# Granule 3's averages transposed by DMA in place of TensorE, granule 7's loads released by these transposes, and steps 8 and 9 reordered

## The chip, the cores and the metric

One core of a Trainium2 chip runs the whole program. The metric is device time in microseconds (us), lower is better. Each execution is listed with its span (first to last event in the trace) and its mean granted TensorE clock. The time is about 1.8 us longer than the span.

## The reference

Attention with a global and a local window and a linear bias, then a two-layer MLP with a squared ReLU:

```python
# q, k, v: (4, 8, 768, 64) fp32, n_global 8, n_local 96
rel = pos[:, None] - pos[None, :]
keep = (pos[None, :] < n_global) | ((rel >= 0) & (rel < n_local))
scores = q @ k.T / sqrt(64) - slope[h] * dist       # -1e9 where not keep
a = softmax(scores)
x = (a @ v) -> (3072, 512)                          # heads side by side
h = x @ w_in                                        # 512 -> 2048
g = s * relu(h)**2 + b
out = g @ w_out                                     # 2048 -> 512
```

## The kernel before

The 3072 tokens go in 12 granules of 256 tokens (2 blocks of 128). A granule needs, in order: loads of k, q, v (GpSimd), their transposes (the first granules on TensorE, the later ones by DMA), scores (TensorE), exponentials (ScalarE), masks (VectorE), attention (TensorE), normalised averages `xn` (VectorE), the averages transposed to `xT`, and the two layers of the MLP. Instructions stand in a hand-written order on each engine; a "step" is half a granule of attention with MLP work of earlier granules mixed in.

`xT` is made in one of two ways, chosen by `X_PE`, and the end of a granule releases the loads of the granule four later:

```python
QK_PE = 4
X_PE = 4          # granules below this: transposes on TensorE
LEAD = 4
...
def x_by_pe(j, evac=(nc.vector.tensor_copy, nc.scalar.copy)):
    t = xT_tile(j)
    for e, ev in enumerate(evac):                      # cut: sizes
        ps = ps_h.tile([P, nk, GT], BF16, name="ps_x", tag="psh")
        ...
        nc.tensor.transpose(ps[:, kc, ...], xn[j][:, i, c : c + P], ident_bf[:])   # 4 per evac
        ev(t[:, e * nk : (e + 1) * nk, :], ps[:])

def x_by_dma(j):
    t = xT_tile(j)
    for i in range(GB):                                # 2
        nc.sync.dma_start_transpose(t[:, :, i * P : (i + 1) * P], xn[j][:, i, :])

def hold_loads(ap):                                    # GpSimd waits until ap is there
    g = work.tile([P, 1], BF16, name="gate", tag="gate")
    nc.gpsimd.tensor_copy(g[0:1, :], ap)

def finish_granule(j):
    if j < X_PE:
        x_by_pe(j)
    else:
        x_by_dma(j)
    while stores:
        stores.pop(0)()
    if 6 <= j + LEAD < NJ:
        hold_loads(xT[j][0:1, 0, GT - 1 : GT])         # the gate
        load_granule(j + LEAD)
```

So the gate of granule 3 is a one-element copy on GpSimd, and everything that GpSimd does after it, granule 7's loads first, waits for `xT` of granule 3. The place of the change in the order of instructions:

```python
make_koff(4)                     # VectorE: shifted keys "ko" of granule 4
run(p1[2][6:8])
finish_granule(3)
run(scores(8))                   # granule 4; half of them read ko
make_voff(4)
p2_mm(2, 0, 0, FC // 2)
...
def step(s, c0, c1, c2, pool=None, pre=()):
    ...
    posts = scores(s + 1)
    run(exps); run(pre); run(masks)
    run(c0)
    stage_A(2 * s); flush()          # attention of two pairs of heads
    ...
    run(c1)
    stage_A(2 * s + 1, pool); flush()
    n = 2 if j < X_PE else 1
    run(c2[0:n])
    if last: finish_granule(j) ...
    run(c2[n:]); flush()
```

`late_p1(3, ...)` and `act_p1(3, ...)` are first-layer groups of granule 3 (8 matmuls, a ReLU on ScalarE, a square on VectorE or, in `act_p1`, on ScalarE). `sg_sum` and `weight_sums` are sums and differences that VectorE prepares for a product scheme with fewer matmuls, `sg_prod` these products.

The softmax here doesn't subtract the row's maximum and nothing guards it: scores larger than these inputs give would overflow.

## Time and profile before

| | before |
|---|---|
| time, median of 3 (lowest to highest) | 207.94 us (207.74 to 208.59) |
| span of the profiled run | 206.1 us |
| TensorE, VectorE, ScalarE, GpSimd busy | 98, 80, 63, 34 % |
| granted TensorE clock | 1.0 |

The prediction shows the busy table, the chain and the queues. Three more things are needed. The first is how busy the 16 DMA engines are over the whole span, in the page's row of 40 slices (5.15 us each, a digit is tenths):

```profile
DMA  5999999999999999999999999994360300340006
```

In the slices up to about 139 us (27 of them, all but the first at 90% or more) DMA has next to no room. The second is the view of the tile `xT` in the kernel before, whose transposes of granules 4 to 11 all go by DMA:

```profile
DMA to landing us min/median/max: 2.4/4.9/8.3
```

The third is the timeline of the kernel before, where the columns are start, busy time, engine, line, operation, and the idle time before it with what ended it. The gate of granule 3 is passed early, and the second attention group of step 10 (line 504) waits 0.24 us for VectorE:

```profile
61.75 0.18 POOL L122 COPY gate<-xT 1x1 bf16<-1x1 bf16 x1
...
81.05 0.29 PEld L504 LDWEIGHTS <-pt 128*128 128x128 bf16 x8 [0.24 <-DVE xn L469]
```

### The profile page before, as it was taken

Reading aid. Unit: us, or ns where it says so; the run is one execution under the profiler, and the core shown is the slowest. Engines: PE = TensorE matmul, PEld = TensorE weight load, DVE = VectorE, ACT = ScalarE, POOL = GpSimd, SP = SyncE. Lnnn points to the kernel's source line nnn. Section 1 sums busy time; section 2 is a strip of 40 time slices with the busy share of each in tenths; the row PEclk is TensorE's granted clock in tenths of the full one; section 3 lists DMA queues with packets and bytes.
Section 4 is the critical chain, followed back from the end, with each engine's and each line's share of the span. In section 5 each row is a group of like instructions: output and inputs, shape, how many; then the busy total and the mean of one; then the engine's idle time right before and its main releaser. Section 6 shows DMA issues by size and latency. Waiting matters only on the chain.

```text
span 206.1 us, 5375 instructions
## 1 busy us (share of the span) xinstructions
PE 201.6 (98%) x2209; PEld 162.5 (79%) x2214; DVE 164.8 (80%) x347; ACT 129.3 (63%) x200; POOL 70.2 (34%) x90
## 2 busy tenths in 40 slices
PE   8999999999999999999999999999999999999993
PEld 2678885557876588888888898888888889888883
DVE  6877689979989999999699865699866696737974
ACT  5767669585975668885763694763694754476200
POOL 8986333899555601808301908200000000000000
PEclk9999999999999999999999999999999999999999
DMA  5999999999999999999999999994360300340006
GB/s 156 177 178 201 207 206 180 155 153 131 126 143 125 156 125 229 117 168 188 145 272 192 131 173 202 180 192 78 54 207 3 101 4 0 69 138 0 3 7 197
DMA packets 110836, 28.17 MB, mean 137 GB/s; under 512 B 97852, under 2 KB 109308, under 8 KB 110812
## 3 DMA queue, kind: packets, MB, share of 16 engines
q0 software_dynamic: 76000, 13.11, 87.9%
q1 hardware_dynamic: 33612, 14.13, 39.9%
q10 hardware_dynamic: 1200, 0.59, 1.1%
q8 instruction: 17, 0.28, 0.5%
q14 instruction: 7, 0.06, 0.1%
HBM read 27.26 MB, written 6.29 MB: 163 GB/s over the span
## 4 chain that ended last, share of the span: by engine, by line
PE 95%; DMA 2%; DVE 0%; ACT 0%; issue 0%
PE ps L632 41%; PE ps L832 24%; PE ps L680 10%; PE ps_s L444 6%; PE ps_av L504 5%; PE ps L968 3%; DMA first<-in_k_dram 2%; PE ps_s L530 1%; PE ps_t L354 1%; PE ps_s L419 1%; PE ps_x L604 1%; PE ps_s L545 1%; PE ps_t L331 1%; PE ps_av L571 1%; PE ps_t L344 0%; PE ps_last L832 0%
## 5 line engine op out<-in xcount | busy, mean ns | idle before, releaser
L632 PE MATMUL ps<-xT,w_in_bf 128*128 128x256 bf16 x768 | 90.4, 273 | 0.0
L642 ACT ACTIVATE gT<-ps 128x512 bf16<-128x512 f32 x96 | 55.8, 598 | 46.0 <-PE ps L632 45.8
L632 PEld LDWEIGHTS <-w_in_bf 128*128 128x128 bf16 x768 | 73.0, 98 | 9.2 <-DVE xT L607 0.2
L453 ACT ACTIVATE pt<-ps_s 128x1024 bf16<-128x1024 f32 (+1 forms) x44 | 39.3, 946 | 2.9 <-PE ps_s L444 2.8
L832 PEld LDWEIGHTS <-gsum 128*128 128x128 bf16 x256 | 24.2, 98 | 3.7 <-DVE gsum L795 0.5
L460 DVE TENSOR_TENSOR pt<-pt,tmpl 128x1024 bf16<-128x1024 bf16 (+1 forms) x40 | 24.4, 644 | 2.1 <-ACT pt L453 2.0
L108 POOL DMA_DIRECT2D vb<-in_v_dram x24 | 21.6, 914 | 5.3 <-DMA w_out_bf<-in_moe_w_out_dram 3.3
L806 DVE TENSOR_TENSOR gT<-gT 128x1024 bf16<-128x1024 bf16 x20 | 13.7, 687 | 11.6 <-ACT gT L642 11.6
L680 PE MATMUL ps<-w_out_bf,gT 128*128 128x512 bf16 x91 | 21.8, 379 | 0.3
L469 DVE TENSOR_TENSOR xn<-ps_av,rc 128x256 bf16<-128x256 f32 x48 | 20.4, 425 | 1.7
L832 PEld LDWEIGHTS <-gT 128*128 128x128 bf16 x200 | 18.6, 98 | 2.3
L504 PEld LDWEIGHTS <-pt 128*128 128x128 bf16 x320 | 14.4, 97 | 2.8 <-DVE xn L469 0.9
L680 PEld LDWEIGHTS <-gT 128*128 128x128 bf16 x96 | 8.9, 98 | 9.6
L468 DVE RECIPROCAL rc<-ps_av 128x4 f32<-128x4 f32 x48 | 8.6, 179 | 9.1 <-PE ps_av L504 7.8
L504 PE MATMUL ps_av<-vb,pt 128*128 128x65 bf16 x208 | 15.5, 193 | 0.0
L832 PE MATMUL ps<-w_out_bf,gsum 128*128 128x256 bf16 x128 | 15.3, 273 | 0.0
L832 PE MATMUL ps<-wsub,gsum 128*128 128x256 bf16 x128 | 15.1, 273 | 0.0
L116 POOL DMA_DIRECT2D nat<-in_q_dram x14 | 12.5, 890 | 6.9 <-DMA nat<-in_q_dram 2.9
L645 DVE TENSOR_TENSOR gT<-gT 128x512 bf16<-128x512 bf16 x30 | 12.2, 421 | 3.2 <-ACT gT L642 2.7
L122 POOL COPY gate<-xT 1x1 bf16<-1x1 bf16 x6 | 1.9, 314 | 36.1 <-DMA xT<-xn 36.1
L116 POOL DMA_DIRECT2D nat<-in_k_dram x14 | 12.6, 900 | 4.7 <-DMA w_in_bf<-in_moe_w_in_dram 2.5
L832 PE MATMUL ps<-w_out_bf,gT 128*128 128x256 bf16 x120 | 13.9, 273 | 0.0
(124 smaller groups left out, 249.7 us busy)
## 6 DMA issues: line engine op xcount, KB each, us to landing
out_dram<-o_q SPq DMA_DIRECT2D x15, 256.0 KB, 2.6
vb<-in_v_dram POOLq DMA_DIRECT2D x24, 128.0 KB, 7.6
nat<-in_k_dram POOLq DMA_DIRECT2D x22, 128.0 KB, 6.8
nat<-in_q_dram POOLq DMA_DIRECT2D x22, 128.0 KB, 6.9
w_out_bf<-in_moe_w_out_dram POOLq DMA_DIRECT2D x4, 512.0 KB, 16.1
w_in_bf<-in_moe_w_in_dram POOLq DMA_DIRECT2D x4, 256.0 KB, 7.6
w_in_bf<-in_moe_w_in_dram POOLq DMA_DIRECT2D x2, 512.0 KB, 11.1
out_dram<-o_sb SPq DMA_DIRECT2D x4, 256.0 KB
```

Of the source, the lines that this page charges most:

```text
L108: nc.gpsimd.dma_start(vbuf[b % 2][:, sb, :, 0:D], rows_of(v, b, sb))
L116: nc.gpsimd.dma_start(t[:, n, i, :, :], rows_of(srcs[n], b, sb))
L444: nc.tensor.matmul(ps[:, hi, oc * P : (oc + 1) * P], lhsT=kt[rows], rhs=qt[rows], start=not bias, stop=not bias or part * GB + n == len(pl ...
L453: nc.scalar.activation(pt[:, :, 0:ncol], ps[:, :, 0:ncol], ACT.Exp, scale=QSCALE)
L460: nc.vector.tensor_tensor(pv, pv, m.rearrange("p h a c -> p h (a c)"), ALU.mult)
L469: nc.vector.tensor_tensor(dst, av[:, :, :, 0:D], rc[:].to_broadcast((P, 2, 2, D)), ALU.mult)
L504: nc.tensor.matmul(av[:, i, hi, 0 : D + 1], lhsT=pt[:, hi, c * P : (c + 1) * P], rhs=vv, start=(n == 0), stop=(n == len(terms) - 1),)
L632: nc.tensor.matmul(ps[:, i, :], lhsT=w_in_bf[:, kc, fc * P : (fc + 1) * P], rhs=xT[j][:, kc, :], start=(kc == 0), stop=(kc == KC - 1),)
L642: nc.scalar.activation(gs, ps[:], ACT.Relu)
L680: nc.tensor.matmul(po[:], lhsT=g_of(j)[:, fc, tb * P : (tb + 1) * P], rhs=w_out_bf[:, fc, :], start=(fc == 0), stop=(fc == FC - 1),)
L806: outs.append(lambda: nc.vector.tensor_tensor(gs, gs, gs, ALU.mult))
L832: nc.tensor.matmul(ps[:, tb, cs], lhsT=stat[:, fc, tb * P : (tb + 1) * P], rhs=mov[:, fc, cs], start=(fc == 0), stop=(fc == NH - 1),)
```

## The change

Intent: TensorE is the bound, so its 8 transposes of granule 3 go to the DMA queue, which serves the later granules already. Because the DMA takes longer, the first-layer groups of granule 3 move from steps 8 and 9 to step 9 alone, and second-layer matmuls of granule 2 fill step 8. The gate then opens only when these transposes have landed.

```diff
-    X_PE = 4
+    X_PE = 3
...
-    step(8, [lambda: rest(2, 0)] + late_p1(3, (0,)), late_p1(3, (1, 2)), late_p1(3, (3,)))
+    step(8, [lambda: rest(2, 0)], [lambda: p2_mm(2, 1, 0, FC // 2)], [lambda: rest(2, 1)])
     step(
         9,
-        [weight_sums[1]] + p2[2][1:2],
-        [sg_sum(3)] + act_p1(3, (4, 5)),
-        late_p1(3, (6,)) + [weight_sums[2]] + late_p1(3, (7,)) + [flush, sg_sum(1)],
+        late_p1(3, (0, 1)),
+        [weight_sums[2]] + late_p1(3, (2, 3)),
+        act_p1(3, (4, 5)) + [flush, sg_sum(3)] + late_p1(3, (6,)) + [weight_sums[1]] + late_p1(3, (7,)) + [flush, sg_sum(1)],
     )
     step(
         10,
         [sg_prod(7), sg_prod(1), sg_prod(2)],
         [bias_diff, lambda: shifted_template(range(H)), sg_prod(5)],
-        [sg_sum(4)],
-        pre=[sg_sum(2)],
+        [sg_sum(4)], pre=[sg_sum(2)],
     )
```

## The prediction

> **What bounds the kernel now.** I read the page's busy table first, then the chain of work that ended last in order of time, then the timeline of single engines around the place that changes, and last the DMA queues there.
>
> ```profile
> PE 201.6 (98%) x2209; PEld 162.5 (79%) x2214; DVE 164.8 (80%) x347; ACT 129.3 (63%) x200; POOL 70.2 (34%) x90
> PE 95%; DMA 2%; DVE 0%; ACT 0%; issue 0%
> ```
>
> TensorE is busy for 201.6 of 206.1 us, and the chain is 95% TensorE: once it has started it hardly waits. So a matmul taken out in the middle is worth its own spacing, and a wait put in costs its own length; nothing downstream gives either back. The chain at the place of the change:
>
> ```profile
> 57.23 1.75 PE ps L632 x16
> 58.98 0.45 PE ps_x L604 x8
> 59.42 0.55 PE ps_s L444 x16
> ...
> 68.61 0.55 PE ps_s L444 x16
> 69.16 0.32 PE ps L680
> ```
>
> The 8 transposes of granule 3 (x8 at 58.98) take 0.45 us of the chain; at once after them come the scores of granule 4 (59.42). The scores of granule 5 stand at 68.61.
>
> The engines that could become the next bound:
>
> ```profile
> 58.62 0.58 DVE L386 COPY ko<-kx 128x1024 bf16<-128x1024 bf16 x1
> 59.24 0.18 DVE L387 COPY ko<-kx 128x64 bf16<-128x64 bf16 x1
> ...
> 59.54 0.27 PEld L444 LDWEIGHTS <-ko 64*128 64x128 bf16 x8
> 59.59 0.39 PE L444 MATMUL ps_s<-qx,ko 64*128 64x128 bf16 x8
> ```
>
> Half of granule 4's scores read the shifted keys (ko), and VectorE finishes those only at 59.42; TensorE takes them up at 59.54. That margin, 0.12 us, is smaller than the 0.45 us to be saved.
>
> The DMA queues, first in 61 to 62, then 66 to 67, then 70 to 71 us (q0 carries GpSimd's loads, q1 the SyncE queue with all DMA transposes; columns are packets, MB, share of 16 engines):
>
> ```profile
> q0 software_dynamic: 477, 0.06, 92.1%
> q1 hardware_dynamic: 398, 0.09, 75.0%
> ...
> q0 software_dynamic: 1228, 0.16, 243.5%
> ...
> q0 software_dynamic: 935, 0.12, 184.2%
> q1 hardware_dynamic: 155, 0.04, 28.9%
> ```
>
> DMA is saturated here. With both queues at work q1 gets about 400 packets a us; alone, q0 moves 1228. q1 falls silent from 66 until some time in 70 to 71: granule 5's last transpose, issued at 58.02, is through by about 65.9, eight us after its issue, and granule 6's first, issued at 66.28, starts after 70.
>
> **What the Trainium skill says.** "DMA: Bandwidth & Descriptors", section "Queues, rings and completion order": each DMA engine goes round-robin between the queue rows that have work, packet by packet. The trace agrees in kind: 398 beside 477 packets in the same microsecond. So the new transposes neither overtake what is in their own queue nor stop the loads. The same page, "Anatomy of one DMA", puts a fixed cost near 2 us on a (GpSimd-issued) transfer, mostly completion. The trace's best SyncE transpose of an xT tile needs 2.4 us from issue to landing, but the median is 4.9 and the worst 8.3, so here queueing decides. "TensorE: Matmul & The Clock Gate", section "Back-to-back issue gap", gives N/2.4 + 2.5 ns, 56 ns for N = 128; the trace shows 0.45 us for 8 transposes, 56 ns each. I therefore count spacing and not the modelled durations of matmul records.
>
> **The change part by part.**
>
> *Removed.* 8 TensorE transposes with their weight loads: 8 x 56 ns = 0.45 us of the chain. Two evacuations of ps_x, one on VectorE (0.42 us at 60.00) and one on ScalarE (0.58 us at 59.51). These two lie beside TensorE work: VectorE waits 0.63 us for ScalarE's exponentials right after, at 61.05.
> How much of the 0.45 us can be had? The scores of granule 4 would start at 58.98, and their ko half at 59.2, but ko is ready at 59.42, and with the usual hand-over TensorE gets on at about 59.5 in place of 59.59. I take a gain of 0.1 us, perhaps 0.15.
>
> *Added.* Two DMA transposes of 128x512 on SyncE. Their source is whole when VectorE has normalised the last pair of heads (57.95 + 0.42 = 58.37), but SyncE is still issuing granule 5's last transpose until 59.83. So they are issued at about 59.9 and 61.2, some 1.3 us each as their neighbours take.
>
> *Moved.* TensorE's order of steps 8 and 9. Before, step 8 held 8 matmuls of the second layer and 4 groups of granule 3's first layer, and step 9 held 16 and 4. After, step 8 holds the 24 second-layer matmuls and step 9 all 8 first-layer groups. A group takes 0.87 us and 8 second-layer matmuls 1.75 to 1.83, so step 8 goes from 1.83 + 4 x 0.87 = 5.3 to 3 x 1.78 = 5.3, and step 9 likewise keeps its length. This is what makes room: the first use of granule 3's averages goes from 64.63 to just behind the scores of granule 5, at 69.16 less the gain, about 69.05.
>
> *Will they have landed by 69.05?* The queue is served in order and is busy until 65.9 with granule 5. Granule 5's first transpose landed at 61.3 (52.7 + 8.6), the last, by the silence of q1, at about 66.7: three in 5.4 us. Of these, one us was a stall in which all of DMA moved next to nothing (63.3 to 64.3 in its view), so beside loads a transpose takes some 4.4/3, 1.5 us. Granule 6's loads go on until about 69, so the two of xT move in 65.9 to 67.4 and 67.4 to 68.9, and completion takes another 0.8: landing at 69.7. The second way: transposes issued at 52.7 and 54.9 landed 8.6 and 7.6 us later; 61.2 plus 8.1 is 69.3. I take 69.5, give or take 0.7. TensorE then waits about 0.5 us: from -0.1 it goes to +0.4 us.
>
> *GpSimd.* It finishes issuing granule 6's loads at about 61.7 and before passed the gate at 61.75, so that granule 7's loads were issued in 62.39 to 70.5, though their data queued behind granule 6's until about 69. With the gate at 69.6 they are issued in 70 to 75.5 and land by about 81 to 82, not 79.5 to 80. The transposes that read them were issued at 79.36 and are used by scores at 101: slack of many us. Only SyncE's order matters: a wait for nat there holds up what is behind, the next of which (xT of granule 5) was issued at 88.25.
>
> *VectorE.* Step 9 gains four squares (4 x 0.4 us) and loses one output (0.74), step 8 the reverse. VectorE is all but full from 70.7 to 84.7. Adding its rows after granule 5's shifted values (about 70.1): masks 1.27, normalise 0.6, two squares 0.8, weight difference 1.2, normalise 0.6, two squares 0.8, sum 0.7, weight difference 1.2, two squares 0.8, two sums 1.4, masks 1.28, normalise 0.6, together 11.2, so the average that frees ps_av for the second attention group of step 10 is done at 81.3 where it was done at 80.99. That group started at 81.05. Thus even without the DMA wait TensorE could not be over 0.25 us early there, rather as much late. The two delays overlap, so I count the larger: +0.4.
>
> *Sum.* -0.45 removed, +0.35 not to be had because of ko, +0.5 waiting for xT: +0.4 us. I add 0.1 for a chance that xT of granule 4 is late too (see below): 207.94 + 0.5 = 208.4 us.
>
> **The rivals.**
>
> 1. *The gain arrives whole or in part.* If the transposes land before 69 (SyncE's issues were quick, the loads give way), the wait is nothing. For it: the schedule was moved to give them 9 us, and landing of most xT tiles took 4.9. Against it: these landed in 75 to 90 us, with queues less full; and ko and VectorE still cap it. 207.5 to 207.9.
> 2. *The transposes land late, 71 to 72.* For it: granule 6's first transpose waited 4 us before it moved a packet, and one transpose of granule 4 took 9.8. Every us late is a us of the total. 209.5 to 210.5.
> 3. *A second wait at granule 4's averages.* They landed at 81.0 and were needed at 82.72. Step 9 ends attention earlier, so they are issued some 0.7 us earlier, but granule 7's loads now stand in their way until 81. I expect 81.6 against a need of about 83.1: no wait, with one chance in five of 0.5 to 1 us.
>
> **Range and chances.** The landing's spread of 0.7 us, cut at zero wait, with rival 3 to the right, gives 207.5 to 209.8. Faster by 2% would need 4.2 us, ten times what was removed; slower by 2% would need xT to land at about 73 or a cascade through the gates. Within 2%: 0.96.
>
> **What would show it.** In the changed profile: the scores of granule 4 begin near 58.98 but their ko half waits on VectorE until 59.5; xT transposes of granule 3 issued at about 59.9 and 61.2, landing near 69.5; a TensorE wait for DMA xT of about half a us at the first L632 group after the scores of granule 5; the gate idle until then, granule 7's loads issued from 70. If TensorE shows no DMA wait and the second attention group of step 10 starts before 80.9, I am wrong on the fast side; if the wait is over 1.5 us or a second one stands at 83, on the slow side.

## The result

The changed kernel took 208.93 us (median of 4, 208.89 to 208.95) beside 207.84 (4 runs, 207.69 to 208.59) of the kernel before on the same chip. The changed kernel's runs were all fast, at a granted clock of 0.997 or more; for the other four the record lists no clock, and all four stand in the ratio. The ratio is 1.0045, with a 95% interval of 1.0021 to 1.0069: 1.09 us longer by the medians. A ratio here and below is the mean time of one kernel's fast runs over that of the other's of the same rounds, so not quite the ratio of the medians that are quoted.

The page of the changed kernel, busy table and chain by engine:

```profile
PE 201.3 (97%) x2201; PEld 161.7 (78%) x2206; DVE 164.3 (79%) x346; ACT 128.8 (62%) x199; POOL 69.6 (34%) x90
PE 61%; DMA 20%; SPq 7%; POOL 5%; DVE 2%; ACT 2%; issue 1%; POOLq 0%
```

TensorE has 8 matmuls less. The chain is no longer TensorE from end to end: followed back it leaves TensorE at granule 3's averages and goes through the DMA queue to the loads. That does not mean that DMA costs 20% of the time; one wait of under 1 us is enough to turn the chain. Its pieces around the change (start, length, what):

```profile
61.14 8.45 DMA xT<-xn
...
74.70 0.61 ACT gT L642
...
75.33 0.63 ACT gT L1047
...
77.48 0.60 ACT gT L642
...
81.80 0.41 PE ps_av L504 x8
```

The transpose takes 8.45 us to land, TensorE goes on at 69.64, and from 74.7 to 81.80 the chain runs first through ScalarE (74.70 to 78.08: ReLUs at line 642 and squares at line 1047), then through VectorE's square, two sums, masks and the average, before it returns to TensorE at line 504. The timeline of the changed kernel, engine by engine:

```profile
59.02 0.18 DVE L387 COPY ko<-kx 128x64 bf16<-128x64 bf16 x1
...
59.25 0.23 PEld L444 LDWEIGHTS <-ko 64*128 64x128 bf16 x8 [0.18 <-DVE ko L387]
...
69.64 1.92 PE L632 MATMUL ps<-xT,w_in_bf 128*128 128x256 bf16 x16 [0.84 <-DMA xT<-xn]
...
70.48 0.87 POOL L116 DMA_DIRECT2D nat<-in_k_dram  x1 [0.61 <-issue]
...
81.80 0.29 PEld L504 LDWEIGHTS <-pt 128*128 128x128 bf16 x8 [0.40 <-DVE xn L469]
...
82.71 0.31 POOL L122 COPY gate<-xT 1x1 bf16<-1x1 bf16 x1 [6.98 <-DMA xT<-xn]
```

Where a figure below has more digits than the views give, it is read from the packed traces. From the same points of TensorE's timeline in both kernels, one profiled run of each, comes an account of where the time went (start in us; e1 is the first experiment, the new order with the old TensorE transposes):

| point on the path | before | after | shift | e1 |
|---|---|---|---|---|
| scores of granule 4 | 59.36 | 58.85 | -0.51 | 59.31 |
| second-layer matmul after them | 59.91 | 59.59 | -0.32 | |
| scores of granule 5 | 68.54 | 68.18 | -0.36 | 68.45 |
| the group after them | 69.09 | 69.64 | +0.55 | 69.01 |
| scores that open step 10 | 76.63 | 77.21 | +0.58 | 76.58 |
| second attention group of step 10 | 81.05 | 81.80 | +0.75 | 81.17 |
| the last long row of first-layer matmuls (96) | 180.15 | 180.88 | +0.73 | 180.26 |
| last VectorE instruction ends | 203.26 | 204.00 | +0.74 | 203.37 |
| end of the span | 206.12 | 207.19 | +1.07 | 206.23 |

So: 0.36 us won at the start; 0.91 lost at the first use of granule 3's averages (from -0.36 to +0.55); 0.17 to 0.20 lost at the second attention group of step 10; nothing in the next 120 us; and 0.33 lost behind the last computation, which nobody had foreseen. The waits of SyncE's own queue at the end show where, for the kernel before and then for the changed one (total us, times, longest):

```profile
SPq L1383 <- DMA out_dram<-o_last: 0.6, 2, 0.3
SPq L1383 <- DMA out_dram<-o_q: 0.4, 1, 0.4
```

```profile
SPq L1382 <- DMA out_dram<-o_last: 1.4, 2, 1.3
```

Behind the last store SyncE passes its end waits one after another, and in these traces always in the same order of semaphores. In the kernel before, the waits pass at 203.68 to 205.21, and the last stores' landings are the last to be asked for. In the changed kernel a landing of the last stores is asked for early: SyncE stands there from 204.42 to 205.72, 1.3 us, and then has seven more waits to pass, the last six 0.06 us apart, to 206.29. The packed traces give the reason: the DMAs that SyncE and ScalarE issue ("hardware DMAs" here) signal eight semaphores in turn. There are 88 of them before and 90 after, so the last store has the last of the eight before, and the second after.

### The profile page after: what moved, and what is told of

It is laid out like the page before. It is cut to its first block, busy times and chain, and to the rows that moved or that the text cites. A ratio compares the mean times of both kernels' runs of the same rounds, so it can differ in the third digit from the quotient of the medians.

```text
span 207.2 us, 5359 instructions
## 1 busy us (share of the span) xinstructions
PE 201.3 (97%) x2201; PEld 161.7 (78%) x2206; DVE 164.3 (79%) x346; ACT 128.8 (62%) x199; POOL 69.6 (34%) x90
## 4 chain that ended last, share of the span: by engine, by line
PE 61%; DMA 20%; SPq 7%; POOL 5%; DVE 2%; ACT 2%; issue 1%; POOLq 0%
PE ps L632 29%; PE ps L832 24%; DMA w_out_bf<-in_moe_w_out_dram 8%; SPq L363 6%; DMA xT<-xn 4%; DMA w_in_bf<-in_moe_w_in_dram 4%; DMA nat<-in_k_dram 3%; PE ps_av L504 3%; PE ps_s L444 3%; POOL nat L102 3%; PE ps L968 1%; POOL vb L108 1%; ACT gT L642 1%; DVE sgsum L943 1%; SPq L612 1%
```

## The experiments

The theory after the result: the loss is (a) the landing of granule 3's transposes, behind granule 6's loads, (b) VectorE's work ahead of the second attention group of step 10, (c) the order of the semaphores at the end. The rivals: the new order by itself costs the time; the late gate (granule 7's loads issued late) costs it. All experiments are variants of the changed kernel unless said otherwise, and all gave correct results. The "tail" is the time from the end of VectorE's last instruction to the end of the span, read from the packed traces. Three calls on three chips; the kernel before took 207.91 (median of 12), 207.72 (11) and 207.79 us (11) there.

### e1: the new order alone

```diff
-    X_PE = 3
+    X_PE = 4
```

> The changed kernel's new order of steps 8 and 9, but granule 3 still transposed on TensorE (and the gate of granule 7 back where it was, since it reads the same tile). My theory: no DMA wait at the first L632 group after the scores of granule 5; VectorE's fuller step 9 makes the second attention group of step 10 start at 81.2 to 81.5 (before 81.05), so 0.1 to 0.4 us slower than before: 207.9 to 208.2 us. Rival (the new order itself costs the time, not the DMA landing): about the changed kernel's 208.9 us.

Measured: 208.04 us (5 runs, 208.00 to 208.09), ratio 1.0006 (0.9993 to 1.0019). The new order alone costs next to nothing, so the first rival falls. The timeline of e1 at the second attention group of step 10:

```profile
81.17 0.29 PEld L504 LDWEIGHTS <-pt 128*128 128x128 bf16 x8 [0.40 <-DVE xn L469]
```

It waits 0.40 us for VectorE as in the changed kernel, without any DMA wait before it, and is 0.12 us later than before, though the scores that open step 10 are 0.05 us earlier: 0.17 us belong to the order.

### e2: the gate at its old time

Granule 7's loads are released by the last average of granule 3, not by its transpose:

```diff
-            hold_loads(xT[j][0:1, 0, GT - 1 : GT])
+            hold_loads(xn[j][0:1, GB - 1, DM - 1 : DM] if j == 3 else xT[j][0:1, 0, GT - 1 : GT])
```

> The changed kernel with granule 7's loads released by the source of granule 3's transposes (ready at 58.4) in place of their landing, so that they are issued from about 62 as before. My theory: the loads queue behind granule 6's until about 69, the transposes land at 69.6 plus or minus 0.3 all the same, the time stays within 0.2 us of 208.9. Rival (the gate protects the transposes): they land at 70.5 or later and the time is 209.7 us or more. Second rival (the late gate costs time further on): under 208.6 us.

Measured: 209.30 us (6 runs, 208.31 to 209.61), ratio 1.0061 (1.0044 to 1.0077). The timeline of e2:

```profile
61.23 0.47 POOL L122 COPY gate<-xn 1x1 bf16<-1x1 bf16 x1
...
70.08 1.92 PE L632 MATMUL ps<-xT,w_in_bf 128*128 128x256 bf16 x16 [0.95 <-DMA xT<-xn]
```

The time lies between the forecast (208.7 to 209.1) and the first rival's 209.7. The gate was passed at 61.23, 8.4 us earlier than in the changed kernel, and nothing was won: the rival that the late gate costs time falls. Nor does the late gate protect the transposes by much: the first use came 0.44 us later than in the changed kernel, while the gated kernels of the same order differ among themselves by more (landings from 68.5 in e7 to 70.0 in e11). A protection of up to 0.4 us stays open.

### e3: a VectorE weight sum moved to where VectorE has room

```diff
-    step(8, [lambda: rest(2, 0)], [lambda: p2_mm(2, 1, 0, FC // 2)], [lambda: rest(2, 1)])
+    step(8, [lambda: rest(2, 0)], [lambda: p2_mm(2, 1, 0, FC // 2)], [weight_sums[1], lambda: rest(2, 1)])
...
-    ... late_p1(3, (6,)) + [weight_sums[1]] + late_p1(3, (7,)) + [flush, sg_sum(1)],
+    ... late_p1(3, (6,)) + late_p1(3, (7,)) + [flush, sg_sum(1)],
```

> The changed kernel with one weight difference (1.2 us of VectorE) moved from step 9 into the 0.9 us in which VectorE is idle in step 8. My theory: VectorE is ready at the second attention group of step 10 about 0.9 us sooner, the weight load there no longer waits for VectorE (0.40 us in the changed kernel), and the group starts some 0.15 us earlier: 208.7 to 208.8 us. Rival (that wait is only a shadow of the late transposes): no change, 208.9 us.

Measured: 209.06 us (5 runs, 208.93 to 209.54), ratio 1.0059 (1.0047 to 1.0071). The expected gain did not come. The timeline of e3:

```profile
77.68 0.91 DVE L645 TENSOR_TENSOR gT<-gT 128x512 bf16<-128x512 bf16 x2 [1.40 <-ACT gT L642]
...
81.85 0.29 PEld L504 LDWEIGHTS <-pt 128*128 128x128 bf16 x8 [0.40 <-DVE xn L469]
```

VectorE now stands idle for 1.40 us before the squares, waiting for ScalarE's ReLU, and the attention group is as late as before. So part (b) of the theory was wrong as stated: it is not the amount of VectorE's work. It is a series that begins at TensorE: first-layer groups of step 9, ScalarE's work on them, the last square, two sums, masks, average, attention. What comes before that square on VectorE does not matter, and the series moves with TensorE.

The delay of 0.17 us in it arises at ScalarE. The last four groups of step 9 and their last ReLUs, in the kernel before and then in the changed one:

```profile
74.79 1.91 PE L632 MATMUL ps<-xT,w_in_bf 128*128 128x256 bf16 x16
76.19 1.14 ACT L642 ACTIVATE gT<-ps 128x512 bf16<-128x512 f32 x2
```

```profile
73.62 3.65 PE L632 MATMUL ps<-xT,w_in_bf 128*128 128x256 bf16 x32
77.01 1.06 ACT L642 ACTIVATE gT<-ps 128x512 bf16<-128x512 f32 x2
```

Before, eight attention matmuls stood between the second and the third of these groups; TensorE ended the last group at 76.70 and ScalarE was through with its ReLU at 77.33, 0.63 us later. In the new order the four groups follow each other, TensorE ends at 77.27, and ScalarE, which has four ReLUs and two squares to do from 74.70 on and pauses for no more than 0.03 us, is through at 78.07, 0.80 us later (in e1 too: 76.65 and 77.45). So the series follows ScalarE's work on the four groups (the chain above leaves TensorE after the first of them) and not the last group alone. This is read from the traces. No experiment gave ScalarE less to do there, for instance by a square moved to VectorE, which stands idle for 1.40 us in e3: that mending is untested.

### e4: the DMA transposes in the order of the kernel before

The kernel before with only `X_PE` changed:

```diff
-    X_PE = 4
+    X_PE = 3
```

> DMA transposes of granule 3 in the old order of steps 8 and 9, where its averages are first needed at about 64.3. My theory: the landing is set by the DMA queues and not by when TensorE asks; it stays near 69.6, TensorE waits about 5.3 us, and the time goes to 212.5 to 213.2 us. Rival (part of the 8.4 us from issue to landing was slack or came from the new order's loads): landing at 67 or before, 210.5 us or less.

Measured: 215.86 us (4 runs, 215.14 to 216.54), ratio 1.0381 (1.0361 to 1.0402). The timeline of e4, then its table of 5-us stretches (stretch, its length, PE busy (count), PEld, DVE, ACT, POOL, granted clock, DMA share, GB/s; the packets' times are added up, so the share can be over 1):

```profile
69.77 1.89 PE L632 MATMUL ps<-xT,w_in_bf 128*128 128x256 bf16 x8 [5.26 <-DMA xT<-xn]
```

```profile
65.00:70.00 5.00, 0.23 (x2) 0.17 (x3) 0.28 (x1) 0.00 (x0) 0.18 (x1) 0.77 1.88 154
70.00:75.00 5.00, 5.00 (x35) 3.77 (x34) 2.79 (x6) 1.19 (x2) 4.37 (x6) 0.55 2.13 147
75.00:80.00 5.00, 4.95 (x48) 2.85 (x48) 4.39 (x11) 3.02 (x4) 0.88 (x2) 1.00 2.32 156
```

The transposes had landed by 69.77, where they land in the changed kernel too: the landing is set by the queue, not by TensorE's order. The wait is 5.26 us, as expected. But the time is 2.7 us above the forecast, and the kernel lost 2.3 us more than the wait: the first use is 5.3 us late (64.47 before), the scores that open step 10 are 7.59 us late (76.63 to 84.22), and 7.58 us remain at the last long row. The reason is the granted clock: after the idle stretch TensorE ran at 0.55 of full speed from 70 to 75 and was back at 1.00 after. The Trainium skill, "TensorE: Matmul & The Clock Gate", section "Part 1: The HAM clock gate", says that the clock is halved after an idle window of some 3.4 us and is full again only after a busy one. The trace agrees: 5.3 us idle, then some 4.5 us at half clock, worth about 2.3 us of work (0.45 x 5 us).

So the new order is what makes the change bearable. It moved the first use from 64.5 to 69.

### e5: the order of semaphores at the end, by itself

The kernel before with two DMAs of 4 bytes that no one reads, late in the kernel:

```diff
+        if j == 9:
+            spare = const.tile([1, 8], F32, name="spare")
+            for i in range(2):
+                nc.sync.dma_start(spare[0:1, i : i + 1], moe_s.to_broadcast((1, 1)))
```

> The kernel before with two DMAs of 4 bytes added on SyncE in a quiet part at about 125 to 145 us, so that the number of DMAs on the hardware queues is that of the changed kernel. In the profiles, from the last VectorE instruction's end to the span's end it is 2.8 us with TensorE transposes (before, first experiment) and 3.2 us with DMA transposes (changed kernel and three experiments), because SyncE waits at the end for eight semaphores in a fixed order and the last three stores then sit on the second and third of them in place of the last ones. My theory: that end grows by 0.3 us here too: 208.1 to 208.3 us, and TensorE's chain is unchanged. Rival (the longer end comes from something the transposes leave behind): 207.9 us, an end of 2.8 us.

Measured: 208.23 us (6 runs, 207.99 to 210.00), ratio 1.0028 (0.9994 to 1.0062): 0.3 us can't be told by time alone. The waits of SyncE's queue at the end of e5:

```profile
SPq L1387 <- DMA out_dram<-o_last: 1.4, 2, 1.3
```

This is the changed kernel's line in the otherwise unchanged kernel. The tail went from 2.86 to 3.21 us. (TensorE's part is not quite unchanged in this profiled run: it waits 0.37 us for queries at 108.07, which the kernel before does not.) Over all traces the tail is 2.83 to 2.86 (before, e1, e8, e10, e11: 88 or 96 hardware DMAs) or 3.19 to 3.21 us (after, e2 to e7, e9: 90), and it is the number of hardware DMAs modulo 8 that sorts them. This settles (c).

### e6: granule 6's loads split, so that the transposes find a shorter queue

Half of granule 6's keys and queries are loaded after granule 2, the rest after granule 3's transposes, and granule 7 goes with granule 8:

```diff
-            load_granule(j + LEAD)
+            if j == 2:
+                load_qk(6, 0)
+            if j == 3:
+                load_qk(6, 1)
+                load_v(6)
+            if j == 4:
+                load_granule(7)
+            if j >= 4:
+                load_granule(j + LEAD)
```

> The changed kernel, but of granule 6's loads only the first two are issued after granule 2; the other four wait for granule 3's transposes, and granule 7's for granule 4's. My theory: the loads' queue is then empty from about 66, the two transposes of granule 3 move uncontended and land at 67.8 to 68.5, TensorE does not wait for them (0.84 us before), and the time falls by 0.7 to 0.9 us against the changed kernel: 208.0 to 208.2 us, if the loads that are put off make no new wait at granule 4's averages (82 us) or granule 6's scores. Rival (the transposes' time is their own and not contention): landing near 69.6, 208.9 us.

Measured: 213.67 us (6 runs, 211.84 to 215.68; two of them slow, left out of the ratio), ratio 1.0243 (1.0201 to 1.0285). The timeline of e6:

```profile
68.31 0.18 POOL L122 COPY gate<-xT 1x1 bf16<-1x1 bf16 x1 [15.29 <-DMA xT<-xn]
...
68.52 1.70 PE L632 MATMUL ps<-xT,w_in_bf 128*128 128x256 bf16 x14
...
95.75 0.57 PE L444 MATMUL ps_s<-qx,kx 64*128 64x128 bf16 x14 [2.94 <-DMA qx<-nat]
```

The first part of (a) is shown here: with fewer loads ahead the transposes landed by 68.31, TensorE took granule 3's averages at 68.52 without a wait, and the scores that open step 10 stood at 76.10, 0.53 us *before* the kernel before. So the removed TensorE work is worth about half a microsecond when the averages are there. But the loads that gave way came back as a wait of TensorE for granule 7's keys and queries: it stood idle for 2.94 us up to 95.75, its weight load waiting for keys up to 93.89 and its matmul for queries after that. I had read from the prediction that they are used at 101; in the kernel before these scores stand at 92.95. Among e6's fast runs the one with a granted clock of 1.000 took 211.84 us, those with 0.992 took 212.82 to 214.11. The profiled run, one of those with 0.992, shows when: the granted clock was 0.62 in 96 to 98 us and 0.52 in 98 to 100, just behind the wait, and 1.00 in the stretches before and after. By these figures that cost some 1.7 us of work (an estimate: 2 x 0.38 + 2 x 0.48). Why one run kept its clock is open.

### e7: sg_sum(2) taken out of the series

```diff
-        [bias_diff, lambda: shifted_template(range(H)), sg_prod(5)],
-        [sg_sum(4)], pre=[sg_sum(2)],
+        [bias_diff, lambda: shifted_template(range(H)), sg_sum(2), sg_prod(5)],
+        [sg_sum(4)],
```

> The changed kernel, but one VectorE sum (0.69 us) goes from before the masks of step 10 to behind the first average of that step. After the last experiment I hold that the wait at the second attention group of step 10 is a series: last group of TensorE's step 9, its relu, square, two sums, masks, average. With one sum out of the series the weight load there should wait no longer for VectorE (0.40 us) and the group start 0.15 us or more sooner against the scores before it: 208.7 to 208.8 us. Rival: no change.

Measured: 209.92 us (6 runs, 208.90 to 210.19), ratio 1.0093 (1.0066 to 1.0121). The timeline of e7's profiled run (the one of 208.90 us):

```profile
82.52 1.05 PE L968 MATMUL ps<-wsub,sgsum 128*128 128x256 bf16 x8 [0.99 <-DVE sgsum L943]
```

The time shows no gain. In the trace the wait at line 504 is gone, which confirms the series, and the product that needs this very sum waits 0.99 us for it instead: the sum can't be put off that far. In this run the transposes of granule 3 were issued at 59.32, 0.45 us earlier than in the changed kernel's trace, and landed at 68.5; TensorE began with them at 68.77, without a wait. Why the five other runs took up to 1.3 us more than the profiled one is open; their clock was 1.0.

### e8: all three mended together

e6, e7, granule 4's shifted keys `make_koff(4)` ahead of a square on VectorE, and six 4-byte DMAs to turn the semaphores (as in e5, with 6 for 2, which makes 8 with the two of the change).

```diff
-    q0()
     make_koff(4)
+    q0()
```

> The loads split, the sum moved, the shifted keys of granule 4 made one VectorE instruction earlier, and six DMAs of 4 bytes in a quiet part so that the last stores sit on the same semaphores as in the kernel before. By my theory the wait for the transposes (0.84), the wait for VectorE (0.15 to 0.2) and the longer end (0.3) are gone and 0.3 to 0.45 us of TensorE's time is saved: 207.4 to 207.6 us, 0.15 to 0.25% under the kernel before. Rival: a new wait in step 11 or 12 for loads put off: 208 us or more.

Measured: 212.07 us (6 runs, 210.93 to 213.85), ratio 1.0207 (1.0164 to 1.0249). The tail was 2.83 us again and granule 3's averages were used at 68.37 without a wait, but TensorE waited 0.99 us for the sum of e7 and 3.08 us, up to 96.54, for granule 7's keys and queries. The rival held: loads put off come back as waits.

### e9: granule 7's loads released by granule 4's averages

e6, with granule 7's loads ahead of the gate of granule 4:

```diff
+            if j == 4:
+                hold_loads(xn[4][0:1, GB - 1, DM - 1 : DM])
+                load_granule(7)
             hold_loads(xT[j][0:1, 0, GT - 1 : GT])
-            load_granule(j + LEAD)
+            if j == 2:
+                load_qk(6, 0)
+            if j == 3:
+                load_qk(6, 1)
+                load_v(6)
+            if j >= 4:
+                load_granule(j + LEAD)
```

> The changed kernel with the last four of granule 6's loads released by granule 3's transposes, as in the split-loads experiment, but granule 7's loads released already when the averages of granule 4 are ready (about 75), not when their transposes have landed (80). My theory: the transposes of granule 3 land near 68.3 and TensorE does not wait; granule 7's keys are there before they are needed at 92.7 (they came at 95.7 in the split-loads experiment, a wait of 3 us); TensorE's chain is 0.3 us shorter than in the kernel before, the end 0.3 us longer: 207.7 to 208.1 us. Rival: the loads now collide with the transposes of granule 4's averages, a wait of 0.5 to 1.5 us at about 82.5: 208.4 to 209.4 us.

Measured: 211.13 us (6 runs, 210.16 to 212.36), ratio 1.0154 (1.0125 to 1.0183). The timeline of e9:

```profile
84.13 0.40 POOL L122 COPY gate<-xT 1x1 bf16<-1x1 bf16 x1 [3.46 <-DMA xT<-xn]
...
116.84 1.92 PE L632 MATMUL ps<-xT,w_in_bf 128*128 128x256 bf16 x16 [1.30 <-DMA xT<-xn]
```

Now granule 4's transposes land just before 84.13, too late for their use (TensorE waits 1.01 us up to 84.14; a VectorE sum, done at 84.03, came no earlier), and granule 6's at 116.8. The rival held again, with the debt one and three granules further on.

### e10: e9 with the other mendings

e9, six 4-byte DMAs, `make_koff(4)` earlier, and in step 10 the masks after the first attention group:

```diff
-        run(masks)
+        if s != 10:
+            run(masks)
         ...
         flush()
+        if s == 10:
+            run(masks)
```

> The same with the shifted keys of granule 4 made one VectorE instruction earlier, the masks of step 10 put behind the first average of that step (so that the second attention group finds its PSUM buffer free), and six DMAs of 4 bytes for the order of the semaphores at the end. By my theory no wait of TensorE above 0.2 us in 58 to 95 us and an end of 2.8 us: 207.2 to 207.5 us, under the kernel before by 0.2%. Rival as above: 208 us or more.

Measured: 210.24 us (6 runs, 209.41 to 212.61, one slow), ratio 1.0114 (1.0079 to 1.0149). The timeline of e10:

```profile
83.14 1.91 PE L632 MATMUL ps<-xT,w_in_bf 128*128 128x256 bf16 x16 [0.98 <-DMA xT<-xn]
...
94.52 0.57 PE L444 MATMUL ps_s<-qx,kx 64*128 64x128 bf16 x14 [0.92 <-DMA qx<-nat]
```

No wait at line 504, the tail at 2.83 us, the first use at 68.43, and still it is slower than the changed kernel: the queue takes it back at granule 4's averages and granule 7's queries.

### e11: the changed kernel with the semaphores turned back

```diff
+        if j == 9:
+            spare = const.tile([1, 8], F32, name="spare")
+            for i in range(6):
+                nc.sync.dma_start(spare[0:1, i : i + 1], moe_s.to_broadcast((1, 1)))
```

> The changed kernel with only the six DMAs of 4 bytes added. By the theory of the end, the three last stores are again on the semaphores that SyncE waits for last, the end falls from 3.2 to 2.8 us and the time by 0.3 us: 208.5 to 208.8 us. Rival: no change, 208.9 us.

Measured: 208.84 us (5 runs, 208.70 to 209.08), ratio 1.0048 (1.0035 to 1.0060). The timeline of e11, then its waits of SyncE's queue at the end:

```profile
70.02 1.16 PE L632 MATMUL ps<-xT,w_in_bf 128*128 128x256 bf16 x9 [1.00 <-DMA xT<-xn]
```

```profile
SPq L1386 <- DMA out_dram<-o_last: 0.7, 3, 0.3
SPq L1386 <- DMA out_dram<-o_q: 0.4, 1, 0.4
```

The end is that of the kernel before (tail 2.83 us, 3.19 in the changed kernel), which gives 0.36 us back. The time hardly shows it, because the transposes landed at 70.0 this time: SyncE was done with issuing them only at 63.8 (60.17 + 3.62), against 62.45 in the changed kernel. At the last long row e11 is 1.10 us behind the kernel before (180.15 to 181.25), and that is its whole loss.

No version beat the kernel before.

## Why the prediction was right or wrong

The time was predicted at 208.4, with 207.5 to 209.8, and measured at 208.93: inside the range, 0.5 us above the centre. The main mechanism was right: a small gain capped by the shifted keys, and a wait of TensorE for transposes that land late behind granule 6's loads. That the total fell inside the range is in part luck: the sum lacked +0.18 us (ScalarE and VectorE in step 10) and +0.33 us (the end), and the range had room to the right for a second wait that did not come. By its own steps:

- **The landing.** Predicted 69.5 give or take 0.7, measured 69.59 (e4: by 69.77). Reading queue silence and the age of neighbouring transposes gave the right number. Other kernels of the same order landed from 68.5 to 70.0. (Rival 1 misread one figure: the transposes with the median of 4.9 us were issued from 75.7 to 176.9 us, not in 75 to 90. Nothing rests on it.) What the prediction had not asked is how SyncE's issuing spreads: the issues ended at 61.97 in e7, 62.45 in the changed kernel and 63.79 in e11, in the order of their landings.
- **The gain capped by ko.** The step said 0.1, perhaps 0.15 us to be had; the trace shows 0.32 to 0.36. It held VectorE's copies to their old time. In the changed trace VectorE finished ko at 59.20, not 59.42, and TensorE's keys were loaded at 59.25. Since other runs of this order took ko as late as 59.55 to 59.59, this gain varies between some 0.05 and 0.35 us.
- **TensorE's wait.** Predicted 0.5, measured 0.84: TensorE came earlier by the gain above, and the landing stayed. The two misses cancel except for 0.15: net +0.4 predicted, +0.55 measured.
- **VectorE and the second attention group.** The average was predicted for 81.3 and was done at 81.74, and the step said that the delays overlap, so only the larger counts. This failed: at that group the shift grew from +0.58 to +0.75. e1 shows the same 0.17 us (from -0.05 to +0.12) without any DMA wait. The step counted VectorE's work and left out ScalarE's, where the delay arises (see e3). e3 and e7 show why it adds instead of overlapping: the series that ends there starts at TensorE's own groups of step 9, so it moves with the wait.
- **GpSimd.** The first load of granule 7 was predicted for 70 and was issued at 70.48. The late gate had no cost (e2). The "slack of many us" was a misreading, 101 for 92.95; it changed nothing here, and tripped e6.
- **A second wait at granule 4's averages.** Predicted at 81.6 against a need of 83.1, with one chance in five of a wait. The gate there opened at 82.71, the need was at 83.47: no wait, with half the margin. e9 and e10 show how near it was.
- **The end.** The step that is missing altogether: +0.33 us by the order of the semaphores, shown by e5 and e11. Without it the time would have been some 208.60.

Sum as measured: -0.36 (removed) + 0.91 (wait), or +0.55; +0.18 (series); +0.33 (end): +1.06, where the two spans differ by 1.07 and the medians of the times by 1.09. The rival that the gain arrives was right about the value of the removed work (e6) and wrong about the queue.

What stays open: the cause of e7's slower runs, what the change costs with less work on ScalarE in step 9, whether the late gate protects the transposes by up to 0.4 us, and why SyncE's issues end up to 1.8 us apart between kernels that are the same up to there.

## What to carry to other kernels

Work moved from the bounding engine to DMA is only free where the queue has room at that time: read the DMA share slice by slice, and estimate a landing from what the queue still holds when the new transfer is issued, not from the median age of a transfer (8.45 us here, against a median of 4.9). When a wait is put into the bounding engine, follow what starts from that engine and returns to it; such a series moves with the wait and its own delay adds; count every engine on it, ScalarE too. And look at the end of the kernel when the number of DMAs changes: 0.33 us here came from no computation at all.

## What the Trainium skill lacked or had wrong

- "Advanced Engine Details and Errata", section "X-Bar Transpose (TRN2)", calls transposing DMAs as fast as regular ones and expects 350 to 400 GB/s. It lacks what one takes in company. Here two 128x512 transposes had landed 8.45 us after the second was issued (61.14), in stretches in which all of DMA moved 126 to 155 GB/s; the best of this shape in the kernel before took 2.4 us, the median 4.9. No run here measures a transpose stream alone.
- No page tells what a kernel's own waits for its last stores cost, or that their order against these stores matters: 2.83 to 2.86 us or 3.19 to 3.21 us from the last computation to the end of the span, at 0.06 us for each passed wait, sorted by the number of hardware DMAs modulo 8.
- "TensorE: Matmul & The Clock Gate", section "Part 1: The HAM clock gate", has the clock fall after an idle window of some 3.4 us; in e6 a wait of 2.94 us was enough (clock 0.62 and 0.52 in the four us from 96 us on), and the fast runs at a mean clock of 0.992 took 1.0 to 2.3 us longer than the one at 1.000. In e4 the 5.3 us of waiting cost 7.6 us in all.
